# All maxima of the first head group ahead of its exponentials, in a fused attention and MLP kernel

## The chip, the core and the metric

The kernel runs on one core of a Trainium2 chip. The metric is device time in microseconds (us), the median of several executions. The engines are TensorE (PE, with its weight loads shown as PEld), VectorE (DVE), ScalarE (ACT), GpSimd (POOL) and SyncE (SP), which here issues every DMA. Each engine runs its own instructions in order; they wait for one another by semaphores.

## What is computed

The reference mixes two branches over the same kind of input, 2048 tokens of width 512, in float32:

```python
def _A_ref(x, wqkv, wo):            # H = 32 heads, Dh = 16, W = 256
    qkv = (x @ wqkv).reshape(B, S, 3, H, Dh).transpose(2, 0, 3, 1, 4)
    q, k, v = qkv[0], qkv[1], qkv[2]
    scores = einsum("bhqd,bhkd->bhqk", q, k) * (Dh ** -0.5)
    mask = (idx[:, None] - idx[None, :] >= 0) & (idx[:, None] - idx[None, :] < W)
    p = softmax(where(mask, scores, -1e9), axis=-1)
    return einsum("bhqk,bhkd->bhqd", p, v).transpose(0, 2, 1, 3).reshape(B, S, D) @ wo

def _B_ref(x, w1, b1, w2, b2):      # F = 1792, gelu by tanh
    return gelu(x @ w1 + b1) @ w2 + b2

g = sigmoid((x * gate_w).sum(-1, keepdims=True))
return g * _A_ref(x, ...) + (1 - g) * _B_ref(x, ...)
```

So each token attends to itself and the 255 tokens before it, and a gate weighs that against an MLP.

## The kernel before

**Dense work.** All large products are made exactly enough by splitting each float32 operand into a high and a low part: `mm3` issues three matmuls of 512 columns for one product (lines 107 to 110). One such triple is a *unit*, planned at `MM3` = 3 x 227 ns. The generator `dense` yields after each unit: first `qkv` for four tiles of 512 tokens (twelve pieces a tile, eight `qk` and four `v`, four units each), then eight turns of `mlp` (`u` pieces with a gelu, then `y` pieces), then `final`. The intermediate queries, keys and values go to DRAM (`SQ`, `SK`, `SV`) and are loaded again in the layouts that attention needs. While a tile's `qkv` runs, its input lies in the buffers that attention uses later: tile 0 in `ks`, tile 1 in `qd`, tile 2 in `qs`. The last tile runs its pieces as four `qk`, four `v`, four `qk`.

**Attention.** The 32 heads are taken in 8 groups of four; a group has 16 blocks of 128 tokens, so 128 blocks in all, counted by `u`. Each block has two kinds of work, four instructions' worth each:

- *Maxima* (`att_max`, line 519 and 524): a matmul of `qd` and `kd` gives the scores of 128 rows in a PSUM tile `sm` (three buffers, tag shared with the input transposes and half of the value products); DVE adds the mask and takes the row maximum into `M`. After four blocks `att_rows` (lines 536 to 546) negates and transposes the 16 columns of `M` on DVE, and eight small casts on POOL write them as extra rows of `qs`.
- *Exponentials* (`att_exp`, lines 564 to 586): a matmul of `ks` and `qs`, whose extra rows subtract the maximum, gives transposed scores in a PSUM tile `st` (three buffers); ACT takes the exponential into `pt`; POOL cuts the band's edges with selects (line 580, four instructions for most blocks, eight for each fourth block; in the last twelve blocks DVE does it).

Each fourth block `att_pvs` (line 608) multiplies the last blocks of `pt` by the values, into one `st` and one `sm` buffer, and ACT and DVE take the sum out. It stands at the third exponential of the following block (`PVAT` = 2).

**The plan.** The program keeps a planned time `now`: `tick` adds the planned ns of PE work, and `after(ns, fn)` puts work of the other engines on a list that is emitted when `now` has passed its due time. `need` brings due work forward. The order in which the functions are called is the order of each engine's queue. `fill(ns)` draws units from `dense` until that many planned ns are used. The order of attention is: `fill(START - AHEAD)`, then the first two `qd` loads, then `fill(AHEAD)`, then the loop over `u` from `-LEAD` to 127. In each step a block of maxima (`m = u + LEAD`) and, from `u = 0`, a block of exponentials is placed, a pair at a time (one at a time in the MLP's `u` stage), and after each a quarter of `STEP0` (for `u < 0`) or of `STEP` is filled with dense units. So the maxima run 12 blocks ahead, and the first exponential comes after START + 12 x STEP0 = 138,000 planned ns of dense work, in the third piece of the first `u` stage.

**Loads.** All go through SP's queue in the order of the calls. `load_kd` and `load_qd` for the next stack of four blocks are called in each fourth step, at the second maximum; the two slots of `kd` and `qd` are used in turn. `load_qs(0, c)` for the first group is called after the maxima of blocks 5, 9, 13 and 17 (`QAT`). `load_ks(0, 0)` and `load_ks(0, 1)` are called after pieces 8 and 9 of tile 2 (line 422); later stacks in the loop. The MLP's weights are loaded one at a time, at most each 4,000 planned ns; 9,000 later ACT copies the high part and DVE or POOL takes the low one (`split`, lines 178 and 182).

Of the kernel before, what the change touches and what calls it, by code (L numbers as in the profile page):

```python
# [19 lines left out]
NT = S // T  # L20
NB = T // 128
# [11 lines left out]
def gated_mix(ctx: ExitStack, tc: tile.TileContext, x, wqkv, wo, w1, b1, w2, b2, gate_w, out):  # L33
# [336 lines left out]
    def qkv(t):  # L370
        last = t == NT - 1
# [29 lines left out]
        for n, (kind, j) in enumerate(pieces):  # L401
            if not last and XAT <= n < XAT + NC:
                nc.sync.dma_start(XT[t][n - XAT], f32(xts[t][:, n - XAT]))
            if kind == "qk":
                need(("w", (kind, j)))
            else:
                need(*[("w", ("v", c)) for c in range(NC)])
            if t == 0 and n == 10:
                nc.sync.dma_start(b1c, b1.rearrange("(f p) -> p f", p=128))
            if t == 0 and n < 2:  # L410
                pass
            elif kind == "qk":
                yield from qkv_qk(t, j)
            else:
                yield from qkv_v(t, j)
            if t == 1 and n % 3 == 2:
                clear_k(n // 3)
            if t == 2 and n < 4:
                clear_q(n)
            if t == 2 and n in (1, 2):  # L420
                load_kd(0, n - 1)
            if t == 2 and n in (8, 9):
                load_ks(0, n - 8)
            if t == 0:
                for i in ([2], [3], [4], [5], [6], [7, 8], [9, 10], [11])[n] if n < 8 else []:
                    split(keys[i], nc.vector if i % 2 else nc.gpsimd)
                if n == 1:
                    after(4000, gate, 0)
                    after(4000, load_xr, 1)
            elif n == 0 and not last:  # L430
                load_xr(t + 1)
            if last and n not in (6, 7):
                load(later.pop(0))
            if last and n == len(pieces) - 1:
                for _ in range(4):
                    load(later.pop(0))
            xat = (5, 7, 8, 9) if t == 0 else (4, 6, 8, 10)
            if not last and n in xat:
                qkv_x(t + 1, xat.index(n))
            if not last and n == xat[-1] + 1:  # L440
                gate(t + 1)
# [18 lines left out]
    def load_ks(g_, c):  # L460


        ready(c, g_, 1)
        n = 2 * NB
        put_pairs([f32(ks[64 * s + 4:64 * s + 52, slot(g_, c)]) for s in range(2)], SK[c], g_)
# [16 lines left out]
    def load_kd(g_, c):  # L482
        for t in range(max(c - 1, 0), c + 1):
            ready(t, g_, 1)
            k0 = 0 if t == c else T - W
            at = W if t == c else 0
            src = heads(SK[t], g_)[:, :, :, :, k0:].rearrange("s d u a c -> (s d u) a c")
            nc.sync.dma_start(f32(kd[0:96, slot(g_, c), :, at:at + T - k0]), src)

    def load_qd(g_, c):  # L490
        ready(c, g_, 0)
        put_pairs([f32(qd[48 * s:48 * s + 48, slot(g_, c)]) for s in range(2)], SQ[c], g_)
# [427 lines left out]
    NU = NG * NKB  # L920
# [2 lines left out]
    for c in (0, 1):  # L923
        load_qd(0, c)
    fill(AHEAD)
    for u in range(-LEAD, NU):
        m = u + LEAD
        gm, bm = divmod(m, NKB)
        step = STEP if u >= 0 else STEP0
        for i in range(4):  # L930
            if i == 1 and m % NB == 0 and NB <= m < NU - NB:
                load_kd(*divmod(m // NB + 1, NT)), load_qd(*divmod(m // NB + 1, NT))
            if i % 2 == 0:
                pair = (i, i + 1) if stage[0] != "u" else (i,)
            elif len(pair) == 2:
                continue
            else:
                pair = (i,)
            for op, i in [(op, k) for k in pair for op in ORDER[:3]] + [("f", k) for k in pair]:
                if op == "s" and u >= 0:  # L940
                    att_exp(u // NKB, u % NKB, i)
                if op == "m" and m < NU:
                    att_max(gm, bm, i ^ XOR)
                if op == "p" and i == PVAT and u >= 1:
                    att_pvs(u - 1)
                if op == "f":
                    fill(step / 4)
        if m < NU and bm % RB == RB - 1:
            after(900, att_rows, gm, bm // RB)
        if m % NB == QAT % NB and QAT <= m < QAT + NKB:  # L950
            load_qs(0, (m - QAT) // NB)
        if u % NB == 0 and NB <= u < NU - NB:
            load_ks(*divmod(u // NB + 1, NT))
        if u % NB == 2 and NB < u < NU - 3 * NB:
            load_qs(*divmod(u // NB + 3, NT))
        if u % NB == 0 and u >= 0:
            att_load_v(*divmod(u // NB, NT))
        if u - NU + NKB in (9, 11, 13):
            load_y((u % NKB - 9) // 2)
# [11 lines left out]
RB = 4  # L971
NKB = S // 128
# [1 line left out]
RAWS = 152000.0  # L974
PUT = 1200
LEAD = 12
QAT = 5
START = 105000.0
NORM = 6000
YSWAP = 3  # L980
GELU = (700, 1500, 3600, 4600, 6000, 7000)
XAT = 3
ORDER = 'mspf'
XOR = 1
PACE = 4000.0
LAND = 7500.0
# [6 lines left out]
DIVS = ((8000, 10000, 16000, 23000, 25000), (4500, 5700, 8500, 17000, 18500))  # L993
REST = 1000.0
MXAT = 5500.0
AHEAD = 9e3
STEP0 = 2750.0
PVAT = 2
STEP = 2330.0
# [20 lines left out]
```

## Time and profile before

| what | value |
|---|---|
| time, median of 3 runs (lowest to highest) | 750.44 us (749.94 to 751.4) |
| the profiled execution's own time, and its span | 750.61 us, 748.9 us |
| granted TensorE clock | 1.00 throughout |
| DMA, mean over the span | 230 GB/s, 172.12 MB moved |
| HBM read and written | 108.53 MB, 62.39 MB |

Times in the views are us from the start of the span; a group of instructions is named by line, engine, operation, output and inputs, then the count, the busy time, the mean of one in ns, and the idle time of its engine just before it with what ended it. PE's instructions overlap, so the spacing of their starts tells their pace, not their length. Which share of the chain that ended last each line has (PE's lines alone):

```profile
PE sm L519 9%; PE st L564 8%; PE pv_sm L608 7%; PE y L108 6%; PE y L109 6%; PE y L110 6%; PE u L108 6%; PE u L109 5%; PE u L110 5%; PE qk L110 4%; PE qk L108 4%; PE qk L109 4%; PE pv_st L608 2%; PE a L108 2%; PE v L108 2%
```

### The profile page before, as it was taken

The page shows a single profiled execution, that of the slowest core. Times are in us where ns is not written, and L with a number is a line of the kernel's source. Part 1 is how long each engine was busy: PE and PEld are TensorE (multiplying, and loading weights), DVE is VectorE, ACT ScalarE, POOL GpSimd, SP SyncE. Part 2 cuts the span into 40 slices and gives each one's busy share as a digit, 9 for nine tenths or more (in the row PEclk, how much of TensorE's full clock was granted, in tenths as well). Part 3 has the DMA queues.
Part 4 walks back from the last instruction along what each step waited for, and adds up shares of the span by engine and source line. Part 5 has one row for each costly group of instructions (what it writes and reads, how often), then busy time and mean ns, then how long its engine had stood idle before and what let it go on. Part 6 is the DMA issues. An engine that isn't in the chain of part 4 may idle for free.

```text
span 748.9 us, 17963 instructions
## 1 busy us (share of the span) xinstructions
PE 734.0 (98%) x6129; PEld 606.7 (81%) x6129; DVE 520.6 (70%) x1567; ACT 421.7 (56%) x972; POOL 372.4 (50%) x846
## 2 busy tenths in 40 slices
PE   9999999998999999999999999999999999999998
PEld 7888888876788888888887887888888888878787
DVE  4532325799768867986798689768867886784552
ACT  4434532358537845764695478447735853784541
POOL 4200000339756865876587567747765875630000
PEclk9999999999999999999999999999999999999999
DMA  9889798997995777799676989996799799438682
GB/s 316 329 268 407 257 392 277 273 312 182 273 251 133 172 229 211 176 227 249 164 174 152 241 215 230 259 235 155 171 268 244 180 238 239 136 88 262 217 287 106
DMA packets 179259, 172.12 MB, mean 230 GB/s; under 512 B 56672, under 2 KB 122976, under 8 KB 179168
## 3 DMA queue, kind: packets, MB, share of 16 engines
q1 hardware_dynamic: 179168, 170.97, 81.3%
q8 instruction: 49, 0.80, 0.5%
q14 instruction: 42, 0.34, 0.2%
HBM read 108.53 MB, written 62.39 MB: 228 GB/s over the span
## 4 chain that ended last, share of the span: by engine, by line
PE 84%; DMA 4%; DVE 4%; ACT 3%; issue 3%; SPq 1%; POOL 1%; DVEq 0%; ACTq 0%; POOLq 0%
PE sm L519 9%; PE st L564 8%; PE pv_sm L608 7%; PE y L108 6%; PE y L109 6%; PE y L110 6%; PE u L108 6%; PE u L109 5%; PE u L110 5%; PE qk L110 4%; PE qk L108 4%; PE qk L109 4%; PE pv_st L608 2%; PE a L108 2%; PE v L108 2%
## 5 line engine op out<-in xcount | busy, mean ns | idle before, releaser
L524 DVE CUSTOM_DVE_ANT_0 jm<-sm,mask 128x320 bf16<-128x320 f32 (+4 forms) x512 | 238.0, 465 | 95.6 <-PE sm L519 61.2
L580 POOL TENSOR_SCALAR_AFFINE_SELECT pt<-pt 64x256 f32<-64x256 f32 (+1 forms) x538 | 228.1, 444 | 108.6 <-ACT pt L586 98.1
L586 ACT ACTIVATE pt<-st 128x320 f32<-128x320 f32 (+4 forms) x512 | 199.6, 424 | 138.7 <-PE st L564 136.1
L519 PE MATMUL sm<-kd,qd 96*128 96x320 f32 (+4 forms) x512 | 154.1, 312 | 6.0 <-DVE M L524 5.1
L564 PE MATMUL st<-qs,ks 128*128 128x320 f32 (+4 forms) x512 | 154.4, 309 | 1.7 <-ACT pt L586 1.7
L546 POOL CAST qs<-tt 4x256 fp32r<-4x256 f32 x256 | 124.2, 485 | 52.7 <-DVE tt L539 42.0
L519 PEld LDWEIGHTS sm<-kd,qd 96*128 96x128 f32 x512 | 96.5, 188 | 32.8 <-DVE M L524 13.5
L564 PEld LDWEIGHTS st<-qs,ks 128*128 128x128 f32 x512 | 97.5, 190 | 18.5 <-ACT pt L586 2.9
L108 PE MATMUL y<-w,h 128*128 128x512 f32 x224 | 88.6, 395 | 0.0
L109 PE MATMUL y<-w,h 128*128 128x512 f32 x224 | 88.1, 393 | 0.0
L110 PE MATMUL y<-w,h 128*128 128x512 f32 x224 | 87.9, 393 | 0.0
L108 PE MATMUL u<-mx,w 128*128 128x512 f32 x196 | 80.0, 408 | 0.0
L109 PE MATMUL u<-mx,w 128*128 128x512 f32 x196 | 77.4, 395 | 0.0
L110 PE MATMUL u<-mx,w 128*128 128x512 f32 x196 | 77.1, 393 | 0.0
L608 PE MATMUL pv_st<-pt,vbuf 64*32 64x320 f32 (+4 forms) x1408 | 73.3, 346 | 1.5 <-ACT pt L586 1.0
L608 PE MATMUL pv_sm<-pt,vbuf 64*32 64x320 f32 (+4 forms) x1408 | 74.2, 347 | 0.2
L608 PEld LDWEIGHTS pv_sm<-pt,vbuf 64*32 64x32 f32 x1408 | 51.2, 106 | 19.3 <-issue 2.2
L325 DVE TENSOR_TENSOR qke<-qk,qke 128x512 fp32r<-128x512 f32 x32 | 22.0, 689 | 46.9 <-ACT qke L322 31.1
L322 ACT ACTIVATE qke<-qk 128x512 fp32r<-128x512 f32 x32 | 19.1, 598 | 56.2 <-PE qk L110 30.3
L110 PEld LDWEIGHTS y<-w,h 128*128 128x128 f32 x224 | 42.1, 188 | 9.8
L608 PEld LDWEIGHTS pv_st<-pt,vbuf 64*32 64x32 f32 x1408 | 46.2, 106 | 1.8 <-ACT pt L586 1.1
L338 POOL MEMSET vx<- 128x32 f32 x16 | 2.4, 155 | 88.9 <-DMA SK<-qke 30.7
(148 smaller groups left out, 1334.7 us busy)
## 6 DMA issues: line engine op xcount, KB each, us to landing
kd<-SK SPq DMA_DIRECT2D x32, 384.0 KB
qs<-SQ SPq DMA_DIRECT2D x64, 192.0 KB
mx<-XT SPq DMA_DIRECT2D x24, 512.0 KB
SQ<-qke SPq DMA_DIRECT2D x16, 512.0 KB
SK<-qke SPq DMA_DIRECT2D x16, 512.0 KB
ND<-nd SPq DMA_DIRECT2D x32, 256.0 KB
raw_w<-in_B_w_dram SPq DMA_DIRECT2D x28, 256.0 KB
ks<-SK SPq DMA_DIRECT2D x32, 192.0 KB
```

The source lines that it names most:

```text
L108: nc.tensor.matmul(p, lh, rh, start=first, stop=False)
L109: nc.tensor.matmul(p, lh, rl, start=False, stop=False)
L110: nc.tensor.matmul(p, ll, rh, start=False, stop=last)
L322: nc.scalar.activation(e[:, h], p, AF.Copy)
L325: nc.vector.tensor_sub(e[:, 1 - h], p, f32(e[:, h]))
L519: nc.tensor.matmul(p[:, :w], qd[0:96, n, pr, 128 * j:128 * (j + 1)], kd[0:96, n, pr, k1 - w:k1], start=True, stop=True)
L524: nc.vector.tensor_tensor_reduce(junk[:, :w], p[:, :w], mask[:, 320 - w:320], 1.0, -3e38, ALU.add, ALU.max, M[:, 2 * (b % RB) + hb, pr:pr ...
L546: nc.gpsimd.tensor_copy(dst, src.unsqueeze(1).broadcast_to([4, 2, RB, 32]))
L564: nc.tensor.matmul(p[:, :w], ks[:, slot(g_, kb // NB), pr, at:at + 128], qs[:, pr, k0:k0 + w], start=True, stop=True)
L580: nc.gpsimd.affine_select(out=v, in_=v, pattern=[[0, v.shape[1]], [1 - 2 * e, 64]], compare_op=ALU.is_ge, fill=0.0, base=-e, channel_multi ...
L586: nc.scalar.activation(pt[:, hf, pr, :w], p[:, :w], AF.Exp, scale=SCALE)
L608: nc.tensor.matmul(pv[r // 64][32 * i:32 * i + 32, q - c * T:e - c * T], vts[g_, b // NB][r:r + 64, v:v + 32], rhs(r), start=start, stop=s ...
```

## The change

The loop's maxima become a function `next_max` that counts them in `made`. START falls from 105,000 to 94,000 and the loop begins at `u = -16` in place of -12, so the first maximum stands 11,000 planned ns of dense work sooner and the first exponential where it was. For `u < 0` all 64 maxima of the first group are placed. For `u >= 0` a maximum is placed only where `made` is behind `4 * (u + 12) + k + 1`: in blocks 0 to 3 none is, and from block 4 the maxima run 12 blocks ahead as before, in the same order within a block.

What goes with it: `att_rows` is called 1,400 planned ns after a group of four blocks' last maximum (before, 900 after the end of that block, whose filling comes after the maximum). The first group's `load_qs` follow blocks 5, 9, 13 and 15, 600 ns after the last maximum. The loads of `kd` and `qd` stand just before the second maximum of their block. `load_ks(0, 0)` and `(0, 1)` move from pieces 8 and 9 of tile 2 to pieces 5 and 6 of the last tile. The first `qd` loads stand 10,000 in place of 9,000 planned ns ahead of the first maximum.

```diff
--- before.py
+++ after.py
@@ -419,8 +419,8 @@
                 clear_q(n)
             if t == 2 and n in (1, 2):
                 load_kd(0, n - 1)
-            if t == 2 and n in (8, 9):
-                load_ks(0, n - 8)
+            if last and n in (5, 6):
+                load_ks(0, n - 5)
             if t == 0:
                 for i in ([2], [3], [4], [5], [6], [7, 8], [9, 10], [11])[n] if n < 8 else []:
                     split(keys[i], nc.vector if i % 2 else nc.gpsimd)
@@ -923,32 +923,39 @@
     for c in (0, 1):
         load_qd(0, c)
     fill(AHEAD)
-    for u in range(-LEAD, NU):
-        m = u + LEAD
+    made = [0]
+
+    def next_max():
+
+        m, i = divmod(made[0], 4)
+        made[0] += 1
         gm, bm = divmod(m, NKB)
+        if i == 1 and m % NB == 0 and NB <= m < NU - NB:
+            load_kd(*divmod(m // NB + 1, NT)), load_qd(*divmod(m // NB + 1, NT))
+        att_max(gm, bm, i ^ XOR)
+        if i == 3 and bm % RB == RB - 1:
+            after(1400, att_rows, gm, bm // RB)
+        if i == 3 and m in QAT:
+            after(600, load_qs, 0, QAT.index(m))
+
+    for u in range(-NKB, NU):
         step = STEP if u >= 0 else STEP0
         for i in range(4):
-            if i == 1 and m % NB == 0 and NB <= m < NU - NB:
-                load_kd(*divmod(m // NB + 1, NT)), load_qd(*divmod(m // NB + 1, NT))
             if i % 2 == 0:
                 pair = (i, i + 1) if stage[0] != "u" else (i,)
             elif len(pair) == 2:
                 continue
             else:
                 pair = (i,)
-            for op, i in [(op, k) for k in pair for op in ORDER[:3]] + [("f", k) for k in pair]:
-                if op == "s" and u >= 0:
-                    att_exp(u // NKB, u % NKB, i)
-                if op == "m" and m < NU:
-                    att_max(gm, bm, i ^ XOR)
-                if op == "p" and i == PVAT and u >= 1:
+            for k in pair:
+                if made[0] < (4 * (u + LEAD) + k + 1 if u >= 0 else 4 * NKB) and made[0] < 4 * NU:
+                    next_max()
+                if u >= 0:
+                    att_exp(u // NKB, u % NKB, k)
+                if k == PVAT and 1 <= u:
                     att_pvs(u - 1)
-                if op == "f":
-                    fill(step / 4)
-        if m < NU and bm % RB == RB - 1:
-            after(900, att_rows, gm, bm // RB)
-        if m % NB == QAT % NB and QAT <= m < QAT + NKB:
-            load_qs(0, (m - QAT) // NB)
+            for k in pair:
+                fill(step / 4)
         if u % NB == 0 and NB <= u < NU - NB:
             load_ks(*divmod(u // NB + 1, NT))
         if u % NB == 2 and NB < u < NU - 3 * NB:
@@ -974,13 +981,12 @@
 RAWS = 152000.0
 PUT = 1200
 LEAD = 12
-QAT = 5
-START = 105000.0
+QAT = (5, 9, 13, 15)
+START = 94000.0
 NORM = 6000
 YSWAP = 3
 GELU = (700, 1500, 3600, 4600, 6000, 7000)
 XAT = 3
-ORDER = 'mspf'
 XOR = 1
 PACE = 4000.0
 LAND = 7500.0
@@ -993,7 +999,7 @@
 DIVS = ((8000, 10000, 16000, 23000, 25000), (4500, 5700, 8500, 17000, 18500))
 REST = 1000.0
 MXAT = 5500.0
-AHEAD = 9e3
+AHEAD = 10e3
 STEP0 = 2750.0
 PVAT = 2
 STEP = 2330.0
```

## The prediction

> **What bounds the kernel now.** I read the page first, then a table by stage, then the waits and the groups of the stage that loses time, and last the timelines of single engines there.
>
> ```profile
> span 748.9 us, 17963 instructions
> ...
> PE 734.0 (98%) x6129; PEld 606.7 (81%) x6129; DVE 520.6 (70%) x1567; ACT 421.7 (56%) x972; POOL 372.4 (50%) x846
> ...
> PE   9999999998999999999999999999999999999998
> ...
> DVE  4532325799768867986798689768867886784552
> ...
> POOL 4200000339756865876587567747765875630000
> ```
>
> TensorE (PE) is busy 98% of the span, so only PE work removed or a PE stall removed can shorten the kernel, and this change removes no PE work. All PE idle time is 748.9 - 734.0 = 14.9 us. The slices 8 and 9 (about 150 to 187 us) are where VectorE (DVE) reads 9 and 9: there the first exponentials meet the first half of the MLP's `u` stage. The table by stage (PE, PEld, DVE, ACT, POOL busy, then clock, DMA share, GB/s) shows the loss:
>
> ```profile
> core 0: us, PE busy (x) PEld busy (x) DVE busy (x) ACT busy (x) POOL busy (x), PEclk, DMA share, GB/s
> 108.50:119.80 11.30, 11.30 (x54) 9.33 (x53) 4.37 (x11) 3.35 (x12) 0.15 (x1) 1.00 0.91 263
> 119.80:150.50 30.70, 30.70 (x149) 25.99 (x148) 22.48 (x88) 9.85 (x28) 8.50 (x17) 1.00 0.93 288
> 160.70:178.90 18.20, 15.64 (x73) 11.53 (x71) 16.91 (x46) 14.58 (x32) 13.06 (x20) 1.00 0.77 195
> 178.90:185.60 6.70, 6.42 (x94) 4.97 (x95) 6.42 (x22) 5.79 (x13) 6.25 (x15) 1.00 1.08 203
> 185.60:193.90 8.30, 7.33 (x39) 6.16 (x38) 7.01 (x23) 5.94 (x14) 7.81 (x15) 1.00 0.72 266
> ```
>
> The maxima that run alone (119.8 to 150.5) cost PE nothing beyond their own time: 30.70 busy of 30.70. The four blocks u=0 to 3 run from 160.7 to 178.9, and PE idles 2.56 us in them. Who is waited for there (window 160.7 to 193.9; total, times, longest), and the groups from 160.7 to 178.9:
>
> ```profile
> PE sm L519 <- DVE M L524: 3.0, 5, 1.0
> PE st L564 <- ACT pt L586: 0.7, 2, 0.4
> ...
> PEld sm L519 <- DVE M L524: 6.4, 12, 1.2
> ```
>
> ```profile
> L586 ACT ACTIVATE pt<-st 128x320 f32<-128x320 f32 x15 | 6.4, 442 | 0.6 <-PE st L564 0.6
> ...
> L524 DVE CUSTOM_DVE_ANT_0 jm<-sm,mask 128x320 bf16<-128x320 f32 x16 | 7.7, 481 | 0.7
> L725 DVE SCALAR_TENSOR_TENSOR sqh<-sqh,x1h 128x512 f32<-128x512 f32 x4 | 3.9, 965 | 0.5 <-ACT sqh L722 0.4
> L737 DVE TENSOR_TENSOR h<-x1h,h 128x512 fp32r<-128x512 f32 x3 | 2.9, 966 | 0.0
> ...
> L519 PE MATMUL sm<-kd,qd 96*128 96x320 f32 (+1 forms) x17 | 5.8, 341 | 1.9 <-DVE M L524 1.7
> L564 PE MATMUL st<-qs,ks 128*128 128x320 f32 x16 | 5.2, 322 | 0.7 <-ACT pt L586 0.7
> ```
>
> The reader is to see that the score matmul of a maximum (`sm`, three PSUM buffers) waits for the DVE reduction (L524) of an earlier one, and that 16 reductions are 7.7 of DVE's 16.91 us. Two rates come from the PE timeline:
>
> ```profile
> 108.41 0.39 PE L108 MATMUL v<-v,qs 128*128 128x512 f32 x1
> ...
> 119.78 0.31 PE L519 MATMUL sm<-kd,qd 96*128 96x64 f32 x2
> ...
> 160.60 0.31 PE L519 MATMUL sm<-kd,qd 96*128 96x320 f32 x1
> 160.75 0.32 PE L564 MATMUL st<-qs,ks 128*128 128x320 f32 x1
> ```
>
> From 108.41 to 119.78 lie 48 dense matmuls and one transpose group: 0.23 us each. An `sm` or `st` takes 0.15 us (160.60 to 160.75). So the 73 matmuls of the four blocks, 33 of them `sm` and `st`, need 40 x 0.23 + 33 x 0.15 = 14.2 us; they took 18.2. The four blocks lose 4.0 us, the only loss that this change aims at directly.
>
> **The change part by part.** *The maxima begin sooner.* START falls by 11,000 planned ns, which is 16 dense units of three matmuls, 48 matmuls: the first `sm` moves from 119.78 to the place at 108.41. Four more blocks of four maxima, 16 x 0.15 = 2.4 us of PE work, now lie ahead of the first exponential, whose place in the dense work stays (12 and 16 blocks of 2,750 planned ns end at the same 138,000). The first `st` comes at 160.75 + 2.4 = 163.15. DVE is busy 4.37 of 11.3 us at 108 to 120, and takes some twelve reductions at most there (6 us): full, but not over. Cost beyond the 2.4: 0.
>
> *The pause.* Blocks 0 to 3 issue no `sm`, so PE needs 14.2 - 2.4 = 11.8 us for them, DVE 16.91 - 7.7 = 9.2 and ScalarE (ACT) the same 14.58. On these three alone the blocks would take between 11.8 and 14.6 us in place of 18.2. That is 1.2 to 4.0 us won, after the 2.4 is paid. But after them comes the first value product (`pv`, in block 4), and it needs the selects (L580) on POOL:
>
> ```profile
> 164.28 1.19 POOL L546 CAST qs<-tt 4x256 fp32r<-4x256 f32 x2 [2.59 <-DVE tt L539]
> 167.44 2.34 POOL L580 TENSOR_SCALAR_AFFINE_SELECT pt<-pt 64x256 f32<-64x256 f32 x4 [1.97 <-ACT pt L586]
> 169.84 3.48 POOL L546 CAST qs<-tt 4x256 fp32r<-4x256 f32 x6
> 173.41 1.29 POOL L182 TENSOR_TENSOR w<-raw_w,w 128x512 fp32r<-128x512 f32 x1
> 174.66 8.68 POOL L580 TENSOR_SCALAR_AFFINE_SELECT pt<-pt 64x256 f32<-64x256 f32 x16
> ...
> 183.27 0.21 PE L608 MATMUL pv_st<-pt,vbuf 64*32 64x64 f32 x1
> ```
>
> POOL works without a pause from 167.44 to 174.66 + 8.68 = 183.34, and the last pair of the first `pv` is issued at 183.27: the selects arrive just in time today. All of that run remains. The eight casts in it are those of the third row group; they move out, but those of the fourth, which stand behind the selects today, move into the same place, since all maxima are done by then. So the question is when this run starts and how long it takes.
>
> *Its start.* It waits for the fourth exponential, 6.7 us after the first `st`. Three reductions stand on DVE ahead of the L737 that frees ACT's next buffer:
>
> ```profile
> 162.17 0.47 DVE L524 CUSTOM_DVE_ANT_0 jm<-sm,mask 128x320 bf16<-128x320 f32 x1
> ...
> 164.07 0.45 DVE L524 CUSTOM_DVE_ANT_0 jm<-sm,mask 128x320 bf16<-128x320 f32 x1
> 164.46 0.76 DVE L737 TENSOR_TENSOR h<-x1h,h 128x512 fp32r<-128x512 f32 x1
> ...
> 165.26 0.69 ACT L719 ACTIVATE x1h<-u,b1c 128x512 f32<-128x512 f32 x1 [1.50 <-DVE h L737]
> ```
>
> Without the three (3 x 0.48) the run starts 5.2 us after the first `st`, at 168.35. Bounds: 6.7 (nothing else helps), and 3.3 (four `st` at the ideal pace, 11.8 / 4 x 3/4 = 2.2, an exponential and the planned 500 ns).
>
> *Its length.* 15.9 us today. It holds 20 selects, and the 64x256 ones are slower here than over the kernel:
>
> ```profile
> L580 POOL TENSOR_SCALAR_AFFINE_SELECT pt<-pt 64x256 f32<-64x256 f32 x334 | 158.3, 494 | 78.7 <-ACT pt L586 72.8
> ...
> L580 POOL TENSOR_SCALAR_AFFINE_SELECT pt<-pt 64x256 f32<-64x256 f32 x12 | 7.7, 666 | 2.2 <-ACT pt L586 2.0
> ```
>
> (the first over the span, the second from 160.7 to 183.5). At the mean of the whole kernel the 12 would be 2.1 us shorter. DVE's L725 and L737 are long as well, 965 and 966 ns, while L524 keeps 481; so it is the gelu's operations and POOL's that lengthen each other, and these stay. I take 14.9, with 13.8 and 15.9 as bounds: PE will stand at the `pv`, no new gelu work comes, and only the last selects run alone. The run ends at 168.35 + 14.9 = 183.25, against 183.34: 0.1 us won.
>
> [...]
>
> *Behind the `pv`.* PE idles 0.97 us in 185.6 to 193.9, behind a DVE that is late. With PE held at the `pv`, DVE has caught up; I take 0.8 back (0 to 1.25, the idle time of both last stages).
>
> *Loads.* `qd`'s first six loads are asked for some 13 us sooner, behind the XT store:
>
> ```profile
> 98.76 0.86 SPq L403 DMA_DIRECT2D XT<-qs  x1
> ...
> 159.80 5.81 DMA qs<-SQ
> ```
>
> At 0.5 to 1.2 us each on SP the first three are out by 101.1 to 103.2; with the 5.81 us of the landing in the chain they are there by 109.0 at the latest, needed at 108.4. I take 0.1 us (0 to 0.6). `ks` (two stacks, six issues) leaves this stretch and goes behind pieces 5 and 6 of the last tile, 24 and 28 units into it, an estimated 134 and 137 us; it is used from 163. `kd`, `qd` and `qs` of later stacks move with their maxima, 13 us sooner, into a stretch with a DMA share of 0.93. What waits behind them on SP are weight loads, which PE needs 20 us later: 0. The row operations are planned up to 0.7 us sooner in the rest of the kernel, with POOL idle time to spare: 0.
>
> **The sum**, against the profiled execution's own 750.61 (span 748.9 and 1.7 around it): 0.1 + 0.8 - 0.1 = 0.8 us won, 749.8; the median shown is 0.17 lower, so 749.6. With the bounds: start 3.3 and length 13.8 give 180.25 (3.1 won, with 1.25 more: 746.1); start 6.7 and length 15.9 give 185.75 (2.4 lost, nothing back, and 0.6: 753.4).
>
> **Rivals.** *1. POOL is not in the way and ACT sets the pace.* The run starts at 3.3 to 4 and the selects fall to their usual mean; PE runs ahead of ACT by its three `st` buffers, 3 x 0.442 = 1.3 us, and the blocks take 14.6 - 1.3 = 13.3: 18.2 - 2.4 - 13.3 = 2.5, with 0.8 behind the `pv` and the 0.1 for the loads 3.2: 747.2. For it: DVE, the releaser named in nearly all waits, loses half its load. Against: POOL's 15.9 us without a gap.
>
> *2. The select run moves along with the exponentials (slower).* Place: POOL, from the fourth exponential of block 0. If that still comes 6.7 us after the first `st` and the run stays 15.9, it ends at 185.75, 2.4 late; 0.8 comes back and 0.1 goes to the loads: 752.1. It decides from a run that ends 2.3 us later than now. For it: none of POOL's work goes. Against: three reductions leave DVE's queue ahead of L737.
>
> *3. The loads crowd.* Weights landing 3 us later would hold ACT's copies in order, and each of some six could cost PE about 0.5 us, 3.0 on top of the forecast: 752.6. Against: PE never waits on a DMA between 119.8 and 150.5.
>
> *4. The change doesn't do what it says*: the lost time is not the maxima's at all, and moves from `sm` to `st` and `pv` to the last tenth: 750.4. Against: the 6.4 and 3.0 us of waits for L524.
>
> **How the numbers follow.** What a measurement of this kernel can tell from no change is about 0.2%, 1.5 us. Forecast 0.42 (0.08 of it faster, 0.30 the same, 0.04 slower); rival 1 0.32, faster; rival 2 0.14 and rival 3 0.08, slower; rival 4 0.04, the same. Faster 0.40, same 0.34, slower 0.26. The forecast's own range is 748.0 to 751.2; to hold 8 in 10 the range reaches to both sides, 746.3 to 752.2.
>
> **What would show it.** Right, if the first `sm` stands near 108.4 without a wait and the first `st` near 163; if no `sm` waits for DVE in blocks 0 to 3, PE's wait is now at the first `pv` for POOL's selects, and POOL's run ends near 183. Wrong, if POOL is done before PE reaches the `pv` (rival 1), or if PE is late ahead of 160 (rival 3).

## The result, and the profile after

| | before | after |
|---|---|---|
| time, median of 6 runs each | 750.86 us (749.94 to 752.12) | 754.77 us (753.61 to 755.62) |
| ratio, 95% interval | | 1.0050 (1.0036 to 1.0065) |
| profiled execution | 750.61 us, span 748.9 | 755.07 us, span 753.4 |
| first `sm` | 119.78 | 108.94 |
| first `st` (block 0) | 160.75 | 165.78, +5.03 |
| first `st` of block 4 | 178.94 | 182.74, +3.80 |
| first `st` of block 8 | 197.16 | 200.18, +3.02 |
| end of the span | 748.90 | 753.36, +4.46 |

The change makes the kernel 0.5% slower; in the two profiles it is 4.46 us. The last four rows of the table say where: 5.03 us are lost ahead of the first exponential, 1.23 come back in blocks 0 to 3, 0.78 behind them, and 1.44 are lost again later, spread over the rest. From the page of the changed kernel, and its table by stage (PE, PEld, DVE, ACT, POOL busy with instruction counts, then granted clock, DMA share, GB/s):

```profile
span 753.4 us, 17968 instructions
...
PE 735.3 (98%) x6129; PEld 608.2 (81%) x6129; DVE 522.7 (69%) x1568; ACT 422.0 (56%) x972; POOL 369.5 (49%) x845
```

```profile
108.50:119.80 11.30, 11.30 (x59) 9.64 (x58) 7.50 (x33) 2.77 (x11) 0.00 (x0) 1.00 0.76 265
119.80:150.50 30.70, 30.37 (x144) 25.26 (x143) 22.98 (x87) 9.16 (x28) 9.40 (x23) 1.00 0.97 289
150.50:165.80 15.30, 14.39 (x68) 11.56 (x67) 13.06 (x45) 6.33 (x11) 4.87 (x10) 1.00 0.94 318
...
165.78:182.74 16.96, 13.61 (x58) 10.64 (x56) 11.78 (x18) 13.96 (x31) 12.69 (x21) 0.90 0.57 153
...
188.60:196.70 8.10, 7.33 (x38) 6.19 (x37) 7.03 (x24) 6.40 (x15) 4.55 (x10) 1.00 1.10 308
```

**Ahead of the first `st`** PE is no longer dense: 0.33 us idle up to 150.5 and 0.91 up to 165.8, where before it idled not at all. The stalls are larger here than these 1.24 us of PE's idle time, since the weight loads around them stop too (PEld waits 2.5 us for reductions in the list below, PE 1.2). Taking for each matmul the time to the start of the next one, over the median of that instruction in the kernel before, PE loses 0.87 us between 100 and 161 before, and 3.14 between 100 and 166 after. So the 5.03 are 2.27 of stalls, 0.53 because the first `sm` starts at 108.94 and not at 108.41, and what is left, 2.23, for the 16 additional maxima (forecast 2.4). The 0.53 is not of the change's making: PE runs without a gap up to the first `sm`, and it is as late from the first `qk` product of the program on (PE's timeline of the changed kernel, then of the kernel before):

```profile
7.16 0.74 PE L310 MATMUL qk<-ks,qk 128*128 128x256 f32 x4 [0.52 <-POOL qk L194]
```

```profile
6.67 0.75 PE L310 MATMUL qk<-ks,qk 128*128 128x256 f32 x4
```

Nothing moved there. The same product starts at 7.15 in e2, whose loads and maxima are those of the kernel before, and at 6.52 in e7, so its place varies from run to run. PE's own rows of waits name only the reduction; the chain behind it goes through two other engines. The waits ahead of the first `st`, from the changed kernel (105 to 166; total, times, longest), then from the kernel before (105 to 161):

```profile
ACT w L178 <- DMA raw_w<-in_B_w_dram: 6.2, 3, 3.8
...
PEld sm L519 <- DVE M L524: 2.5, 4, 1.2
...
DVE qke L325 <- ACT qke L322: 1.7, 1, 1.7
PE sm L519 <- DVE M L524: 1.2, 2, 0.9
```

```profile
ACT w L178 <- DMA raw_w<-in_B_w_dram: 0.4, 1, 0.4
```

The timelines of ACT, DVE, and PE in the changed kernel around the largest of these:

```profile
149.66 0.63 ACT L178 ACTIVATE w<-raw_w 128x512 fp32r<-128x512 f32 x1 [3.78 <-DMA raw_w<-in_B_w_dram]
150.20 0.58 ACT L322 ACTIVATE qke<-qk 128x512 fp32r<-128x512 f32 x1
...
150.81 0.69 DVE L325 TENSOR_TENSOR qke<-qk,qke 128x512 fp32r<-128x512 f32 x1 [1.69 <-ACT qke L322]
151.42 0.48 DVE L524 CUSTOM_DVE_ANT_0 jm<-sm,mask 128x320 bf16<-128x320 f32 x1
...
151.97 0.42 PE L519 MATMUL sm<-kd,qd 96*128 96x320 f32 x1 [0.85 <-DVE M L524]
```

ACT stands 3.78 us at the copy of a weight that has not landed. The eviction of `qk` (L322) is queued behind it; DVE's half of that eviction (L325) waits for it, the next reductions (L524) are queued behind L325, and the `sm` waits for the reduction. Nobody needs that weight yet. Why it is late is seen on SP's queue, in the changed kernel and then in the kernel before:

```profile
136.13 0.59 SPq L170 DMA_DIRECT2D raw_w<-in_B_w_dram  x1
136.76 0.55 SPq L480 DMA_DIRECT2D ks<-SK  x1
...
145.54 0.37 SPq L477 DMA_DIRECT2D ks<-SK  x1
145.96 0.43 SPq L170 DMA_DIRECT2D raw_w<-in_B_w_dram  x1
```

```profile
132.45 0.59 SPq L170 DMA_DIRECT2D raw_w<-in_B_w_dram  x1
137.94 0.43 SPq L170 DMA_DIRECT2D raw_w<-in_B_w_dram  x1
```

The fifth and the sixth weight are issued at 132.45 and 137.94 before, at 136.13 and 145.96 after. The copy's place in ACT's order follows from the plan, not from the issue. Which of the loads that were moved makes the weights late was not isolated (e4 and e7 below).

**In blocks 0 to 3** no `sm` waits any more, and yet they take 16.96 us, with no engine full. Part of it is the TensorE clock, 0.90 in the row above: from 177.65 us on it is granted at half for 3.41 us (see the last section). Half of that, an estimated 1.7 us, is added to PE's busy time; without it the 13.61 would be 11.9. The timelines of DVE, ACT, PE, POOL:

```profile
168.22 0.45 DVE L539 STREAM_TRANSPOSE tt<-nm 128x256 f32<-128x256 f32 x1
168.59 0.65 DVE L737 TENSOR_TENSOR h<-x1h,h 128x512 fp32r<-128x512 f32 x1
...
169.28 0.69 ACT L719 ACTIVATE x1h<-u,b1c 128x512 f32<-128x512 f32 x1 [1.55 <-DVE h L737]
...
171.44 0.42 PE L564 MATMUL st<-qs,ks 128*128 128x320 f32 x1 [1.19 <-ACT pt L586]
...
176.74 0.38 PE L564 MATMUL st<-qs,ks 128*128 128x320 f32 x1 [2.16 <-ACT pt L586]
...
171.47 2.74 POOL L580 TENSOR_SCALAR_AFFINE_SELECT pt<-pt 64x256 f32<-64x256 f32 x4 [1.53 <-ACT pt L586]
174.27 2.88 POOL L546 CAST qs<-tt 4x256 fp32r<-4x256 f32 x5
...
180.04 6.55 POOL L580 TENSOR_SCALAR_AFFINE_SELECT pt<-pt 64x256 f32<-64x256 f32 x12
```

POOL's run starts 5.69 us after the first `st` and lasts 15.1 us, to 186.59. PE waits for the exponential, and the exponential stands on ACT behind an L719 that waits for DVE's L737: 1.55 us the first time, 0.55 the second, where the copy of a weight and two more operations of the gelu follow ahead of the exponential. The first of these L737 stands on DVE behind the last reduction of the first group (167.21) and the three row operations of its fourth row group (167.73 to 168.67). Three reductions had left that place; this work came to stand there.

**Later** the value products wait for a reduction where before they waited for none. DVE and PE at block 39 of the changed kernel, then of the kernel before:

```profile
334.85 0.27 DVE L536 TENSOR_SCALAR nm<-M 128x16 fp32r<-128x16 f32 x1
335.15 0.21 DVE L537 SCALAR_TENSOR_TENSOR nm<-M,nm 128x16 fp32r<-128x16 f32 x1
335.46 0.45 DVE L539 STREAM_TRANSPOSE tt<-nm 128x256 f32<-128x256 f32 x1
335.83 0.45 DVE L524 CUSTOM_DVE_ANT_0 jm<-sm,mask 128x320 bf16<-128x320 f32 x1
...
336.35 0.30 PE L608 MATMUL pv_sm<-pt,vbuf 64*32 64x64 f32 x2 [0.58 <-DVE M L524]
```

```profile
332.47 0.49 DVE L524 CUSTOM_DVE_ANT_0 jm<-sm,mask 128x320 bf16<-128x320 f32 x1
332.89 0.17 DVE L536 TENSOR_SCALAR nm<-M 128x16 fp32r<-128x16 f32 x1
...
332.64 0.24 PE L608 MATMUL pv_sm<-pt,vbuf 64*32 64x64 f32 x1
```

The row operations now stand ahead of the last reduction of the block, which frees the PSUM buffer that the `pv` takes; before they stood behind it.

### The profile page after: what moved, and what is told of

It is laid out like the page before. It is cut to its first block, busy times and chain, and to the rows that moved or that the text cites. A ratio compares the mean times of both kernels' runs of the same rounds, so it can differ in the third digit from the quotient of the medians.

```text
span 753.4 us, 17968 instructions
## 1 busy us (share of the span) xinstructions
PE 735.3 (98%) x6129; PEld 608.2 (81%) x6129; DVE 522.7 (69%) x1568; ACT 422.0 (56%) x972; POOL 369.5 (49%) x845
## 4 chain that ended last, share of the span: by engine, by line
PE 76%; DVE 9%; DMA 6%; issue 5%; ACT 3%; SPq 1%; POOL 0%; DVEq 0%; ACTq 0%; POOLq 0%
PE sm L519 8%; PE st L564 8%; PE pv_sm L608 6%; PE u L108 6%; PE y L108 6%; PE y L109 5%; PE y L110 5%; PE u L109 5%; PE u L110 5%; DVE jm L524 4%; PE qk L110 3%; PE qk L108 3%; PE qk L109 3%; PE pv_st L608 2%; PE a L108 2%
## 5 line engine op out<-in xcount | busy, mean ns | idle before, releaser
L524 DVE CUSTOM_DVE_ANT_0 jm<-sm,mask 128x320 bf16<-128x320 f32 (+4 forms) x512 | 238.2, 465 | 97.8 <-PE sm L519 62.0
L546 POOL CAST qs<-tt 4x256 fp32r<-4x256 f32 x256 | 121.5, 475 | 58.9 <-DVE tt L539 28.9
L608 PEld LDWEIGHTS pv_sm<-pt,vbuf 64*32 64x32 f32 x1408 | 52.0, 106 | 20.1 <-DVE M L524 3.7
L325 DVE TENSOR_TENSOR qke<-qk,qke 128x512 fp32r<-128x512 f32 x32 | 22.1, 690 | 44.3 <-ACT qke L322 32.6
L110 PEld LDWEIGHTS y<-w,h 128*128 128x128 f32 x224 | 42.0, 188 | 9.8
L322 ACT ACTIVATE qke<-qk 128x512 fp32r<-128x512 f32 x32 | 19.1, 598 | 51.6 <-PE qk L110 29.6
L108 PEld LDWEIGHTS y<-w,h 128*128 128x128 f32 x224 | 42.4, 189 | 3.7
```

The costliest lines, as they stand in the source:

```text
L108: nc.tensor.matmul(p, lh, rh, start=first, stop=False)
L110: nc.tensor.matmul(p, ll, rh, start=False, stop=last)
L322: nc.scalar.activation(e[:, h], p, AF.Copy)
L325: nc.vector.tensor_sub(e[:, 1 - h], p, f32(e[:, h]))
L524: nc.vector.tensor_tensor_reduce(junk[:, :w], p[:, :w], mask[:, 320 - w:320], 1.0, -3e38, ALU.add, ALU.max, M[:, 2 * (b % RB) + hb, pr:pr ...
L546: nc.gpsimd.tensor_copy(dst, src.unsqueeze(1).broadcast_to([4, 2, RB, 32]))
```

## The experiments

The time of the kernel before ranged over 3 to 7 us within each set of these runs, so the ratios are read with their intervals, and where 1 us or less decides, the profile. "Shift" is the start of a block's first `st` less that of the same block in the kernel before.

**e1 and e2: the place of the row operations.** In e1 they are put back, in e2 the kernel before gets the new place alone.

```
-        if i == 3 and bm % RB == RB - 1:
-            after(1400, att_rows, gm, bm // RB)
+        (after the block's last fill)  after(900, att_rows, gm, bm // RB)
```

> The changed kernel, with the row operations (L536 to L539) asked for 900 planned ns after the end of a block, as before the change, and not 1400 after its last maximum. Theory (the three row operations now stand on VectorE ahead of reductions that the next value product's PSUM buffer waits for): the waits pv_sm L608 for the reduction (1.5 us in 4 waits in the changed kernel's profile) vanish, the first blocks stay as they are, and the end comes 1.0 to 1.5 us sooner: 753.3 to 753.8 beside 754.8. Rival (the drift of 1.4 us behind block 39 comes from something else, such as the clock or the loads): 754.5 to 755.0, and the waits turn up elsewhere.

> The kernel before, with only the row operations asked for 1400 planned ns after the group's last maximum. Theory: it alone costs 1.0 to 1.5 us, so 751.8 to 752.4 beside 750.9, with new waits of pv_sm for the reduction. Rival (harmless by itself): 750.5 to 751.2.

Measured: e2 1.0016 (1.0001 to 1.0031) to the kernel before; e1 1.0041 (1.0028 to 1.0055). The waits between 300 and 640 us of e2, then of e1:

```profile
PE sm L519 <- DVE M L524: 3.0, 5, 1.1
PE pv_sm L608 <- DVE M L524: 1.4, 3, 0.6
PE pv_st L608 <- ACT pt L586: 0.7, 1, 0.7
PE sm L519 <- DVE nd L632: 0.4, 1, 0.4
```

```profile
PE sm L519 <- DVE M L524: 3.2, 6, 1.1
PE pv_st L608 <- ACT pt L586: 0.7, 1, 0.7
PE sm L519 <- DVE nd L632: 0.4, 1, 0.4
```

The wait is there with the new place and gone with the old one. In e2 the shift rises by 0.71 at block 41, 0.27 at 73, 0.34 at 89 and 0.30 at 105, 1.6 us in all; in e1 it falls against the changed kernel at the same four blocks by 0.73, 0.35, 0.36 and 0.33. That part of the loss is settled. e1's time does not show all of it: in its profile a weight was 5.8 us late, and the first `st` 1.34 us behind that of the changed kernel. The size of the stalls ahead of the first `st` varies from run to run.

**e3, e4, e7: the late weights.** e3 puts the copies 3,000 planned ns later in ACT's order; e4 puts the `ks` loads back; e7 puts off `kd`, `qd` and `qs` loads that nothing needs yet.

```
e3  -  after(LAND + 1500, split, ...)        +  after(LAND + 4500, split, ...)
e4  -  if last and n in (5, 6):              +  if t == 2 and n in (8, 9):
e7  m == 12: after(14000, load_kd / load_qd); load_qs after 600, 600, 8600, 16600
```

> The changed kernel, with the split (ScalarE's copy L178 and the subtraction behind it) of the weights that are loaded ahead of 152,000 planned ns put 3,000 planned ns later in the order; the loads stay where they are. Theory (late weights hold ScalarE in order, then VectorE, then TensorE): ScalarE's waits for raw_w (6.2 us in 3 waits between 105 and 166) fall under 1.5 us, the two sm waits near 152 vanish, and the first st comes 1 to 2 us sooner than its 165.8; the end 752.8 to 753.8. Rival (the stall ahead of the first st is VectorE's own load of reductions): first st within 0.4 of 165.8 and the time 754.4 to 755.2, with the sm waits where they were.

> The changed kernel, with k's first stacks (ks) asked for behind pieces 8 and 9 of the third tile, as before the change. Theory (the six ks issues stand on SP's queue ahead of the weights, 136.8 to 145.5 us, and make them late): the weights land 2 to 4 us sooner, ScalarE's waits for raw_w fall under 2 us, and the first st comes 1 to 2 us sooner, so 752.8 to 753.8. Rival (the new place of ks is innocent; it is kd, qd and qs of the later stacks, or ks now holds up qd's first loads near 100 to 108): first st at 165.8 or later, 754.6 or more, and a wait of the first sm for qd.

> The changed kernel, with the loads that the early maxima drag along but that nothing needs before 175 us put off: kd and qd of the second head group's first stack by 14,000 planned ns, qs of the third and fourth tile by 8,000 and 16,000. ks stays where the change put it. Theory (the loads of later stacks crowd out the weights on a full DMA, 0.95 to 0.97 of it between 120 and 166; ks alone was not it): ScalarE's waits for raw_w between 105 and 166 fall from 6.2 us to under 3, PE loses 1.5 us or more less ahead of the first st than its 3.1, and the time falls to 752.8 to 754.0. Rival (only weights issued behind 156 us gain, those at 146 to 153 stand behind ks, kd and SV): the loss ahead of the first st stays at 2.5 to 3.5, and the time at 754.3 to 755.2, or the blocks 0 to 3 alone win up to 1.

| | ratio, 95% | PE's loss ahead of the first `st` | first `st` | blocks 0-3 | shift at block 8 |
|---|---|---|---|---|---|
| changed kernel | 1.0050 (1.0036 to 1.0065) | 3.14 | 165.78 | 16.96 | 3.02 |
| e3 | 1.0035 (1.0023 to 1.0046) | 1.60 | 164.27 | 18.08 | 2.78 |
| e4 | 1.0054 (1.0040 to 1.0069) | 3.75 | 166.07 | 16.72 | 3.61 |
| e7 | 1.0051 (1.0035 to 1.0068) | 2.72 | 164.72 | 17.03 | 2.04 |

e3 confirms the chain: with the copies later, the stalls of the changed kernel at 150.8 and 153.6 are gone and the first `st` comes 1.5 us sooner. But the same copies then stand ahead of exponentials, one of which waits 4.6 us behind a weight (the wait list from 105 to 200):

```profile
PE st L564 <- ACT pt L586: 4.7, 2, 4.6
ACT w L178 <- DMA raw_w<-in_B_w_dram: 3.2, 2, 1.8
```

e4 missed: without `ks` in that place the copies wait more, 11.6 us in seven waits; `ks` at its old place delays what follows on SP just as well, and the sixth weight is issued at 145.91 (145.96 in the changed kernel). e7 missed too: its raw waits are 7.8 us, and of its 1.06 us at the first `st` 0.67 are an earlier first `sm`, which is the start of the program again.

**e5, e6, e8, e9: what sets blocks 0 to 3.** e5 gives five copies to VectorE; e6 leaves the pause out; e8 is e5, e7 and e1 together; e9 leaves out POOL's selects of blocks 0 to 3.

```
e5  138000 < now < 156000:  -  nc.scalar.activation(w[:, 0], raw, AF.Copy)   +  nc.vector.tensor_copy(w[:, 0], raw)
e6  -  LEAD = 12             +  LEAD = 16
e9  -  else:  (selects)      +  elif g_ or kb > 3:
```

> The changed kernel, with the first step of the weight splits between 138,000 and 156,000 planned ns (ScalarE's copy L178, five of them between about 164 and 187 us, 0.63 us each) done by VectorE's tensor_copy. Theory (in blocks 0 to 3 of the changed kernel ScalarE sets the pace: 13.92 of 16.9 us busy, st waits for the exponentials 3.3 us; the select run on POOL follows its sixteenth exponential): the blocks take 14.5 to 15.5 us in place of 16.9, the last select ends 1 to 2 us sooner after the first st than the changed kernel's 20.8, and the shift at u=8 falls by 1 to 2 us; the time 752.8 to 754.0. Rival (POOL's run of casts and selects has its own length): the last select still ends 20.3 to 20.9 after the first st, and the time is 754.4 to 755.2. Rival (late landing of the weights): VectorE now waits for raw_w in order and the blocks take 17 or more.

> The changed kernel with LEAD 16: the maxima begin as early, but don't pause and stay 16 blocks ahead of the exponentials to the end (the last 16 blocks' masks are done on VectorE in place of 12). Theory (the pause is what won 1.3 us in blocks 0 to 3, and behind the pv 0.8): blocks 0 to 3 take 18 us or more with sm waits for VectorE again, the shift against the kernel before is near 5 at the first st and stays there or grows, so 755.5 to 757.5. Rival (the pause wins nothing, ScalarE and POOL set the pace either way): blocks 0 to 3 take 16.5 to 17.3 and the time is that of the changed kernel, 754.3 to 755.3.

> The changed kernel with three edits at once: the copies of those weights on VectorE, the later loads, and the row operations 900 planned ns after a block's end as before the change. Theory (the loss has the three places: weights ahead of the first st, ScalarE in blocks 0 to 3, rows from block 40 on): 2 to 4 us under the changed kernel, 750.8 to 752.8, so level with the kernel before or within 2 us of it. Rival (each of them only moves the wait): over 753.5.

> The changed kernel without the mask selects (L580, POOL) of the first head group's blocks 0 to 3: 20 of POOL's instructions are left out and the masked corners keep their exponentials. Theory of the prediction (POOL's run of selects sets when the first pv can end): the pv no longer waits for POOL, the shift at u=8 falls from 3.0 to 1.0 or less, the time to 752.5 to 753.2. Theory after the experiments so far (ScalarE and VectorE set the pace through the gelu's buffers, in-order: x1h L719 waits for h L737 and st for the exponential; POOL follows 3.3 us behind the sixteenth exponential): the sixteenth exponential still ends 17 to 17.9 us after the first st, and only what lies behind it, 0.3 to 1.2 us, is won: 753.5 to 754.6. If POOL's reads are what stretch VectorE's gelu operations (0.8 to 0.9 us, one of 1.52), these fall to 0.7 and the sixteenth exponential comes 1 us sooner.

e5: 1.0061 (1.0042 to 1.0080), blocks 0 to 3 in 17.95 us and not 14.5 to 15.5: taking the copies from ACT and giving them to DVE does not shorten them. e8, which has the same copies, 1.0048 (1.0032 to 1.0064), blocks in 17.60; its three edits together missed the 750.8 to 752.8 expected (755.00). e6: 1.0112 (1.0093 to 1.0130); its blocks take 17.73 us with `sm` waits again, so the pause does save there, but most of its loss, from a shift of 5.9 at block 8 to 11 at block 74, comes in the rest, where the lead is longer; it was not taken apart. e9: 1.0044 (1.0028 to 1.0061), and its window of blocks 0 to 3:

```profile
164.75:182.19 17.44, 14.46 (x57) 11.27 (x56) 10.93 (x19) 14.41 (x33) 6.24 (x9) 0.80 0.56 156
```

With POOL's load halved (6.24 us) the blocks are no shorter, and the sixteenth exponential ends 18.2 us after the first `st` (17.6 in the changed kernel). The first `st` was 1.03 us sooner than in the changed kernel, 0.48 of it by an earlier first `sm`, the shift at block 8 only 0.36 smaller. But this is no clean test of the selects: in this profile the clock is granted at half for 6.83 us of these blocks (0.80 in the row), in the changed kernel for 3.41 (0.90). Half of the difference, an estimated 1.7 us of PE's work, can hide what leaving the selects out gives. What the changed kernel's own profile shows is that no matmul waits for POOL between 105 and 200 us. The last select ends at 186.59, and the last products of the first `pv` are issued at 186.64 to 186.67, just in time, as in the kernel before; it ends 3.2 to 3.3 us behind the sixteenth exponential before and after. What fits e5 is the order of waits above: `st` waits for an exponential, which stands behind an L719, which waits for L737 or for a `u` that stands behind that `st`. That this loop alone sets the 17 us was not tested, nor was a third `x1h` buffer, which would loosen it.

**e10, e11, e12: weights in time.** The first MLP weights are asked for closer together, and copied later, so that the copies do not move on into the exponentials. e11 and e12 add e7's loads and e1's rows; in e12 the closer spacing holds for the early weights alone.

```
-  paced[0] = max(now[0], paced[0] + PACE)                  (PACE 4000)
+  e10, e11: PACE 2800        e12: 2800 if now[0] < 130000 else PACE
-  after(LAND + 1500, split, ...)    +  after(LAND + 4000, split, ...)
```

> The changed kernel with the first MLP weights asked for 2,800 planned ns apart in place of 4,000, and copied 11,500 planned ns behind their load in place of 9,000. Theory (a weight's issue falls behind the plan on SP's queue, the one at 146 us by 8 us against the kernel before, and ScalarE waits for it in order): the copies' waits for raw_w fall from 6.2 us to under 2, PE loses under 2 us ahead of the first st in place of 3.1, and the first st stands at 164.0 to 164.8; blocks 0 to 3 stay at 16.5 to 17.3; the time 753.0 to 754.0. Rival (as with the copies put later alone: what is won ahead of the first st is lost in blocks 0 to 3): first st near 164.3, blocks 18, the time 754.2 to 755.

> The same edit of the weights, with the later loads of e7 and the row operations 900 planned ns behind a block's end. Theory (three places, which add up): no pv_sm wait for the reduction behind block 40 (1.4 less drift), first st at 163.5 to 164.8, the time 751.2 to 752.8, so about the kernel before. Rival (they only move waits): 753.5 or more.

> As e11 (weights sooner and copied later, later loads, rows as before), but the closer spacing of 2,800 planned ns holds only for loads asked for ahead of 130,000 planned ns; all later weights keep 4,000. Theory (the new sm waits of e10 and e11 between 425 and 475 us come from the closer spacing of the later weights): first st at 163.2 to 164.8, no raw_w wait over 1.5 us ahead of it, no drift between blocks 41 and 120 against the kernel before, 751.2 to 753.0. Rival (those waits vary from run to run in any kernel): a drift of 1 us or more near block 66 again, 753 to 755.

| | ratio, 95% | median | first `st` | shift at block 4 | at 8 | at 56 | at 120 |
|---|---|---|---|---|---|---|---|
| e10 | 1.0072 (1.0049 to 1.0095) | 756.95 | 163.60 | 1.33 | 2.12 | 3.26 | 4.79 |
| e11 | 1.0042 (1.0025 to 1.0059) | 755.08 | 163.39 | 0.54 | 1.97 | 2.01 | 3.82 |
| e12 | 0.9995 (0.9985 to 1.0004) | 750.56 | 163.69 | 1.44 | 1.55 | 1.52 | 1.60 |
| e15, changed kernel again | 1.0064 (1.0049 to 1.0080) | 755.54 | 166.09 | 4.07 | 3.31 | 3.98 | 6.04 |

Three stages of e12 up to its first `st`:

```profile
108.50:119.80 11.30, 11.30 (x60) 9.59 (x59) 7.42 (x32) 2.85 (x12) 0.00 (x0) 1.00 0.78 274
119.80:150.50 30.70, 30.70 (x148) 25.96 (x147) 24.51 (x92) 9.44 (x28) 11.31 (x23) 1.00 0.94 285
150.50:163.69 13.19, 13.19 (x63) 10.96 (x63) 10.67 (x37) 5.40 (x9) 3.14 (x8) 1.00 0.82 281
```

PE is dense again, and the first `st` stands 54.67 us behind the first `sm`: 52.34, which the kernel before needs from 108.41 to its first `st`, and 2.4 for the maxima make 54.74. (The first `sm` stands at 108.29 in e10, 108.64 in e11, 109.02 in e12 and 109.07 in e15; the first `st` and the shifts of the table move with it.) e12 keeps the early maxima and the pause and has the time of the kernel before; with e15 on the same chip the edits take off 0.7%. e10 and e11 missed in time, though their first `st` is as early. Their profiles lose 0.4 us near block 51, which e11 gets back by block 53, and 0.7 (e10) and 1.8 (e11) between blocks 64 and 72. A stall of 1.1 to 1.3 us near block 66 is also in the profiles of e1, e2, e14 and e15, which keep the old spacing, and not in those of e12 and e13, so it is partly an accident of a run; what the closer spacing of the later weights costs beyond that was not settled.

**e13, e14, e15.** e13 is e12 with the casts of the fourth row group 10,000 planned ns later; e14 is e12 without the selects of blocks 0 to 3; e15 is the changed kernel.

> As e12, with POOL's casts of the first head group's fourth row group (L546) 10,000 planned ns later, behind the selects of blocks 0 to 3. Theory (once the weights are in time, POOL's run sets the pv: in e10 and e11 pv waits 1.1 us for the selects and the last select ends 22.2 to 22.7 after the first st): the last select ends 20.8 to 21.8 after the first st, the pv's waits for POOL vanish, and the shift at u=8 is 0.5 to 1.5 less than that of e12. Rival (the sixteenth exponential sets it): the last select ends as in e12 within 0.4, the time too.

> As e12, without the mask selects of the first head group's blocks 0 to 3 (the masked corners keep their exponentials). Theory (POOL takes back what weights in time win): the shift at u=8 falls 1.5 or more below that of e12, where in the changed kernel the same edit won 0.4 on top of its earlier first st's 1.0, that is nothing behind it; the pv waits for no POOL work. Rival (ScalarE's order takes it back): the shift at u=8 within 0.5 of that of e12.

> The changed kernel itself once more, on the chip of these runs, as their base: a ratio of 1.0036 to 1.0065 to the kernel before, the first st 4 to 6 us later than in the kernel before, and ScalarE waiting 4 us or more for raw_w ahead of it. If the late landing were an accident of the one profile, the first st would stand near 163.2 and ScalarE's waits under 2 us.

e15 repeats the finding: first `st` 5.34 us later than before, ACT waits 6.6 us for raw weights, the same three copies. e13 0.9996 (0.9974 to 1.0017), e14 1.0001 (0.9986 to 1.0015). In e13's profile the last select ends 18.7 us after the first `st` (21.6 in e12) and the shift at block 8 is -0.29, 1.84 less; 0.7 of it goes at block 12, where an `st` waits for `ks`, and the median is no better than e12's. Part of the 1.84 is no work of the casts: 0.35 is an earlier first `sm`, and in e13 no weight was over 0.6 us late, in e12 one was 2.2. The wait lists put the second wait of an `st` in these blocks down to a cast (L546), 2.4 us of PE in e12 and 2.6 of PEld in the changed kernel; but an exponential ends there in the same 0.3 us, and in e13, where no cast stands there, the same `st` waits 2.4 us for the exponential alone. In e14 the shift at block 8 is 0.71 less than in e12, between the two theories, and neither profile has a halved clock there: once the weights land in time, the selects hold up the first `pv` a little (PE waits 0.5 us for them in e12, 1.1 in e10), and cost a part of what was won, not all. No version beat the kernel before by more than its interval.

## Why the prediction was wrong

It forecast 749.6, range 746.3 to 752.2; 754.77 was measured. By its own steps, on the profiled spans:

- **"Cost beyond the 2.4: 0" and "What waits behind them on SP are weight loads, which PE needs 20 us later: 0"** are the step that failed. They cost 2.27 us in stalls. It is true that PE needs those weights later; ACT meets them first, in an order written for weights that land sooner, and what stands behind ACT's copy is PE's own way on. The price was in the text as rival 3 (752.6 with a chance of 0.08): its mechanism is the one found, three copies late where it had six. Its "Against", that PE never waits on a DMA between 119.8 and 150.5, looked at the wrong engine: PE does not wait on a DMA in the changed kernel either. With the weights in time (e12) the rest of the step was right: the first `st` at 163.69, forecast 163.15, with a first `sm` that is 0.61 late from the start of the program.
- **"The row operations are planned up to 0.7 us sooner ...: 0"** failed. It named POOL as the cover; the operations also move past reductions on DVE, and cost 1.44 us (e2 alone: 1.6 in the profile).
- **Loads of `qd`: 0.1** was not too small: PE is dense up to the first `sm`, which waits for no load. It starts at 108.94, not 108.41, because the whole program started 0.5 us later in this profile; the sum compares single profiles and has no term for that.
- **The run of selects.** Start 5.69 us after the first `st` (forecast 5.2), length 15.1 (14.9), end 20.8 (20.1): the numbers held within 0.7. The reason did not: POOL was taken for what holds the `pv`, and PE's wait was to be there; in the changed kernel PE's matmuls wait for the exponentials in blocks 0 to 3, and for POOL nowhere. Once the weights are in time the selects do hold the `pv` a little (e12, e14). That the gelu's operations and POOL's lengthen each other is in the trace of the changed kernel: L725 at 165.76 takes 1.52 us beside POOL's L182 (165.29, 1.45 us), and 0.69 at 171.13, where POOL's select at 171.47 takes 0.62 us in place of the 0.41 that most of them take. Over its whole span L725, L731 and L737 take at most 0.69 us where no instruction of POOL runs beside them and up to 1.52 where one does; the 64x256 selects take at most 0.42 us where DVE runs nothing but L524 beside them and up to 0.96 beside those three; the 128x320 reductions of L524 take at most 0.49 us either way. Why was not shown.
- **0.8 behind the `pv`**: counted from the last select, which comes 3.26 us later than before (186.60 against 183.34), to block 8 (3.02), 0.24 us were won. VectorE was late there in spite of the pause: PE still idles 0.77 us in the stage behind the `pv` (0.97 before).
- **No `sm` waits in blocks 0 to 3** held, but not "between 11.8 and 14.6": the blocks took 16.96. PE idles 3.35 us in them behind exponentials, and the halved clock, for which the forecast had no term, adds the estimated 1.7. The "1.2 to 4.0" won was counted after the 2.4 were paid; counted so, 1.2 are lost here. The forecast's sum went by the selects instead, so it carries only part of this, in the next line.

Summed: 2.53 more up to the first `st` (2.27 of stalls and 0.53 of the start, less 0.17 that the maxima and 0.1 that the loads cost less than forecast), 0.72 less won up to the last select, 0.56 less behind it, and 1.44 in the rest are 5.25 us between the forecast gain of 0.8 and the loss of 4.46.

## What to carry to other kernels

A transfer that is moved ahead of others on a queue is paid by whoever waits for the others first, and here that was not the engine that uses the data, PE, but one that prepares it and works in order (ACT waits 6.2 us for raw weights ahead of the first `st`, PE for none): follow the late transfer to the first instruction that reads it, then to what is queued behind that. When work is asked for by planned time, a shift of 0.7 us in the plan can swap its place with an instruction that the bound engine waits for (1.6 us in e2's profile); compare the order on every engine it passes. And price a pause together with what it concentrates elsewhere: here 16 maxima moved ahead cost 2.2 to 2.3 us and won back 2.0 by block 8 in the changed kernel, 1.4 in e12, so even with both losses mended it came out level. Before a term of a forecast is called wrong by half a microsecond, look where two profiles first part: here that was at 7 us, before anything that was moved.

## What the hardware showed that was not expected

In the changed kernel the TensorE clock is granted at half for 3,413 ns, from 177.65 to 181.06 us. PE's timeline shows it at work: the same matmuls follow each other in 0.23 us, then in 0.43.

```profile
176.96 0.40 PE L108 MATMUL u<-xt,w 128*128 128x512 f32 x1
177.19 0.40 PE L109 MATMUL u<-xt,w 128*128 128x512 f32 x1
...
177.91 0.63 PE L108 MATMUL u<-xt,w 128*128 128x512 f32 x1
178.34 0.63 PE L109 MATMUL u<-xt,w 128*128 128x512 f32 x1
```

Counted from the start of each profile's clock record, the halving begins at a whole number of times this length (49, 50, 51 in e4, the changed kernel, e1). PE's idle time in the 3,413 ns just ahead of a halving, and, in profiles without one between 165 and 195 us, the largest in any such stretch, counted off in the same way:

```
halved:      e4 1.76  e5 1.76  e9 1.89  e8 1.99  e7 2.15  changed 2.16  e1 2.16  e15 2.16  e10 2.17  e3 3.41
not halved:  before 0.97  e2 0.90  e6 0.79  e13 1.29  e14 1.51  e12 1.67  e11 1.83
```

e8 also has a stretch of 1.71 without a halving, just ahead of the one with 1.99. So among these figures 1.89 us or more stands ahead of a halving each time and 1.71 or less never; between them 1.76 (e4, e5) does and 1.83 (e11) does not. e12 has a gap of 2.42 us, 1.27 of it in one stretch and 1.15 in the next, and keeps its clock. In e9 the halving lasted two stretches, 6.83 us. That the idle time is what halves the clock was not shown.

What the halving costs was not settled. A mean clock of 0.998 or less, which one such halving gives (0.998 in the profile of the changed kernel), is in 10 of the 12 runs of the changed kernel (with e15) and in 17 of the 87 of the kernel before, so it is more frequent with the change. Blocks 0 to 3 take 16.67 to 18.08 us in the profiles of the pause that have it and 15.03 to 16.69 in those without (e11 to e14), but these have their weights sooner, too. In time it does not stand out: the changed kernel's runs with a mean clock of 1.0 took 755.09 and 753.61 us, those with 0.997 or 0.998 754.33 to 755.62.
